# Transposing k, v and r by DMA instead of by matmuls from the fifth chunk on, with the instruction order drawn up anew

One core of a Trainium2 chip. The metric is the device time of one execution in microseconds (us), lower is better. Runs are compared with runs of the kernel before on the same chip. A run is called slow when it is over 1.5% above the fastest run of its kernel, otherwise fast; medians below are over all runs, ratios over fast ones alone. The engines: PE does the matmuls, DVE, ACT and POOL the element-wise work and the copies, SP issues DMAs.

## What is computed

A linear-attention recurrence with a 40x40 state for each of 4 x 8 heads over 768 steps, followed by an MLP with a softplus on the 3072 resulting rows of 320:

```python
for t in range(S):                       # r, k, v, w, a, b: [4, 8, 768, 40] f32
    y[:, :, t] = einsum('bhd,bhde->bhe', r[t], state)
    Sa    = einsum('bhde,bhe->bhd', state, a[t])
    state = state * w[t][..., None] - einsum('bhd,bhe->bhde', Sa, b[t]) \
                                    + einsum('bhd,bhe->bhde', v[t], k[t])
x = y.transpose(0, 2, 1, 3).reshape(3072, 320)
out = softplus(x @ w_in) @ w_out         # w_in 320x2048, w_out 2048x320
```

The kernel works in 12 chunks of 64 steps. In a chunk the recurrence becomes products of 64x64 blocks ("grams"), a triangular inversion (by DVE or POOL, one for two chunks) and a short chain on the state; the MLP of a chunk follows when its y is there.

## The kernel before

A small list scheduler in the program orders all operations by due times ("TUNED") on a cost model and then emits them, one in-order stream for each engine. The cut shows one chunk's transposes. `op(engines, reads, writes, fn)` enters an operation; `evac` copies PSUM to SBUF on ACT or DVE, whichever the scheduler picks.

```python
def transpose(src, srcs, t, off):            # 8 transposing matmuls of 128x128 into PSUM
    def f(e):
        for bp in X2:
            for yy in range(H_ // 2):
                i = T.transpose(pb(t)[:, bp, off + 128*yy:off + 128*yy + 128],
                                src[:, bp, 128*yy:128*yy + 128], ident[:, :])
        return i
    return op(pe(8 * 56.0), srcs + ["ident"], [t], f, mode=FULL, name="tr")
...
for n, dst, dn in (("v", v_, vn), ("r", r_, rn)):          # POOL casts f32 to bf16
    op(pool(640 * 0.85), landed(RAW[n], c), [dn], ...)
t = Tile("a")
transpose(k_, [kn], t, 0)
transpose(v_, [vn], t, 512)
evac(1024, [t], [kTn], lambda t=t: kT_[:], ...)
evac(1024, [t], [vTn], lambda t=t: vT_[:], ...)
t = Tile("a")
transpose(r_, [rn], t, 0)
evac(1024, [t], [rTn], lambda t=t: rT_[:], ...)
masked(grams(kT_, kTn, G, aT_, aTn, F), ta[:], tan)        # first readers
masked(grams(vT_, vTn, G, rT_, rTn, G), p_[:], pn)
...
op({"sp": 200.0}, [on], [...],                             # stores and most loads: SP
   lambda e, ...: S.dma_start(out[row:row + L, :], ot[q:q + 64, :]), ...)
```

kT, vT, rT and r_b have one buffer each, v_b two.

Of the kernel before, what the change touches and what calls it, by code (L numbers as in the profile page):

```python
# [17 lines left out]
NEAR = 4  # L18
GT = 8
DVE_FW = (0, 1)  # L20
FIRST = ["b2", "w0", "a0", "b1", "w2", "a1", "a2", "r3", "v3", "r1", "k0", "v2", "a3", "b3", "v1", "k2", "k1", "r0",
    "k3", "v0", "r2", "b0"]
BY_ACT = ("a2", "b0", "b1", "b2", "k3",)

DUE = {}
TUNED = {("const", 0): (-3.693, 1.677), ("logs", 0): (-8.629, 903.459), ("logs", 2): (3.218, 2.271),
    ("logs", 4): (9.161, 0.555), ("logs", 6): (1.81, 0.029), ("logs", 8): (3.58, 3.191),
    ("logs", 10): (1.467, 0.43), ("first", 0): (-6.199, 0.211), ("first", 1): (-2.981, 1.025),
    ("first", 2): (-2.078, 0.185), ("first", 3): (-1.533, 0.02), ("first", 4): (-3.465, 0.201),
    ("first", 5): (-3.012, 0.221), ("first", 6): (-3.897, 2.263), ("first", 7): (-3.262, 0.329),  # L30
    ("first", 8): (-1.395, 0.039), ("first", 9): (-5.529, 0.956), ("first", 10): (-1.743, 0.114),
    ("first", 11): (-2.881, 0.778), ("invert", 0): (-10.218, 0.059), ("invert", 1): (-5.518, 0.024),
    ("invert", 2): (-7.57, 0.518), ("invert", 3): (-3.213, 0.079), ("invert", 4): (-5.511, 0.134),
    ("invert", 5): (-2.481, 13.837), ("weights", 0): (1.187, 928.349), ("csb", 0): (0.548, 691.95),
    ("before", 0): (-5.516, 0.172), ("before", 1): (-0.859, 0.024), ("before", 2): (0.018, 0.026),
    ("before", 3): (0.176, 0.59), ("before", 4): (0.665, 1.484), ("before", 5): (0.314, 0.462),
    ("before", 6): (-3.434, 2.547), ("before", 7): (4.711, 1.26), ("before", 8): (1.286, 1.509),
    ("before", 9): (0.234, 0.102), ("before", 10): (-0.599, 50.77), ("before", 11): (-7.144, 0.037),
    ("W", 0): (11.058, 0.094), ("W", 1): (0.162, 0.089), ("W", 2): (3.065, 0.189), ("W", 3): (-2.415, 81.382),
    ("W", 4): (-4.831, 6.172), ("W", 5): (0.114, 0.183), ("W", 6): (-0.851, 0.546), ("W", 7): (11.05, 12.868),  # L40
    ("W", 8): (1.208, 0.442), ("W", 9): (-3.367, 3.578), ("W", 10): (3.873, 0.948), ("W", 11): (1.626, 0.28),
    ("chain", 0): (0.366, 0.103), ("chain", 1): (0.823, 0.27), ("chain", 2): (0.607, 0.021),
    ("chain", 3): (0.517, 0.239), ("chain", 4): (0.917, 0.02), ("chain", 5): (0.415, 0.364),
    ("chain", 6): (0.982, 0.194), ("chain", 7): (2.773, 0.063), ("chain", 8): (-0.307, 0.235),
    ("chain", 9): (-0.166, 1.763), ("chain", 10): (2.249, 0.247), ("chain", 11): (-1.862, 7.214),
    ("after", 0): (0.576, 0.02), ("after", 1): (-0.482, 1.399), ("after", 2): (0.383, 0.189),
    ("after", 3): (-3.78, 1.371), ("after", 4): (-7.952, 3.19), ("after", 5): (-2.305, 0.052),
    ("after", 6): (-4.679, 0.366), ("after", 7): (-0.275, 0.048), ("after", 8): (-0.196, 0.697),
    ("after", 9): (-3.747, 4.706), ("after", 10): (-1.685, 1.926), ("after", 11): (10, 1.373),
    ("mlp", 0): (0.936, 0.072), ("mlp", 1): (1.107, 1.432), ("mlp", 2): (0.768, 1.497),  # L50
    ("mlp", 3): (1.021, 1.422), ("mlp", 4): (0.453, 0.271), ("mlp", 5): (-0.453, 2.276),
    ("mlp", 6): (0.981, 0.601), ("mlp", 7): (1.01, 1.599), ("mlp", 8): (-2.424, 0.838),
    ("mlp", 9): (-2.927, 0.024), ("mlp", 10): (-6.757, 17.608), ("mlp", 11): (-3.21, 0.023),
    ("load w", 4): (-8.02, 13.468), ("load w", 6): (-4.853, 7.506), ("load w", 8): (-3.389, 9.625),
    ("load w", 10): (-5.349, 0.02), ("load a", 4): (2.419, 0.02), ("load a", 5): (5.777, 0.056),
    ("load a", 6): (-3.318, 0.081), ("load a", 7): (-0.465, 0.024), ("load a", 8): (-0.222, 0.269),
    ("load a", 9): (2.558, 1.896), ("load a", 10): (-5.461, 0.023), ("load a", 11): (0.774, 0.989),
    ("load b", 4): (-7.204, 0.118), ("load b", 5): (-0.103, 0.077), ("load b", 6): (-7.078, 0.203),
    ("load b", 7): (-2.54, 0.02), ("load b", 8): (-1.682, 0.02), ("load b", 9): (0.892, 6803.691),
    ("load b", 10): (-7.568, 0.102), ("load b", 11): (-8.196, 123.948), ("load k", 4): (-4.002, 0.086),  # L60
    ("load k", 5): (-5.178, 0.02), ("load k", 6): (-5.609, 0.045), ("load k", 7): (-7.576, 0.02),
    ("load k", 8): (-4.291, 0.278), ("load k", 9): (0.319, 112.278), ("load k", 10): (-3.896, 0.021),
    ("load k", 11): (-3.756, 1.782), ("load v", 4): (-0.823, 1.073), ("load v", 5): (-1.083, 0.84),
    ("load v", 6): (0.068, 1502.815), ("load v", 7): (-4.848, 1195058.862), ("load v", 8): (3.334, 2.238),
    ("load v", 9): (5.232, 4.558), ("load v", 10): (-3.373, 1248.895), ("load v", 11): (1.415, 186.217),
    ("load r", 4): (-1.133, 1.48), ("load r", 5): (-2.972, 0.39), ("load r", 6): (5.651, 4.768),
    ("load r", 7): (3.08, 0.625), ("load r", 8): (-1.475, 18.071), ("load r", 9): (6.571, 43.008),
    ("load r", 10): (9.094, 1220.994), ("load r", 11): (1.725, 0.138)}
NQ = DFF // 128
LN2 = 0.6931471805599453  # L70

# [92 lines left out]
LAT = {"pe": 240.0, "dve": 130.0, "act": 150.0, "pool": 130.0, "sp": 0.0}  # L164
SELF = 75.0
SWITCH = 150.0
PEN = 14.64
PERIOD = 25000.0
BETA = 0.29


BLOCK, AHEAD, FETCH, BEFORE = 256, 82, 2300.0, 70

PORT = ("scale", "fw")
SLOW = ("h", "o", "csb")
FILL, SAVE, MARGIN = 10072.17, 241245251.54, 6.88
COUNT = {"tr": 8, "tot": 16, "gram": 32, "cum": 8, "W": 32, "X1": 16, "X": 32, "D": 32, "U": 32,
         "S1": 4, "S": 64, "sT": 32, "y1": 16, "y": 64, "yT": 6, "h": 6, "o": 4, "csb": 16}

# [209 lines left out]
def bass_rwkv7_goose__then__act_softplus_kernel(  # L389
# [17 lines left out]
    with ExitStack() as st:  # L407
# [32 lines left out]
        def pb(t, lo=0, hi=1024):  # L440
            return psb[:, t.bank:t.bank + 2, lo:hi]
# [51 lines left out]
        csb = sb("csb", [128, DM], F32)  # L493
# [40 lines left out]
        def evac(cols, reads, writes, o, i, fast=False, name="", only=None):  # L534

            c = dict(dve(cols * (0.52 if fast else 1.04)))
            c.update(act(cols))
            if only:
                c = {only: c[only]}
            return op(c, reads, writes, lambda e: copy(e, o(), i()), name=name)  # L540
# [152 lines left out]
        def transpose(src, srcs, t, off):  # L693
# [4 lines that stand above are left out]
                        i = T.transpose(pb(t)[:, bp, off + 128 * yy:off + 128 * yy + 128],  # L698
                                        src[:, bp, 128 * yy:128 * yy + 128], ident[:, :])
                return i  # L700
            return op(pe(8 * 56.0), srcs + ["ident"], [t], f, mode=FULL, name="tr")

        def at(side, bp, x, yy):

            return bp, 128 * yy + side(bp, x)
# [87 lines left out]
        def first(c):  # L793
# [18 lines left out]
               lambda e: V.scalar_tensor_tensor(hd(n_), bh(bf_, D_), -1.0, bh(gi, D_), ALU.mult, ALU.mult), name="scale")  # L812
            op(dve(666), landed(RAW["k"], c) + [gin], [kn],
               lambda e: V.tensor_tensor(hd(k_), bh(kf, D_), bh(gi, D_), ALU.mult), name="scale")  # L814
            t = Tile("a")
            transpose(a_, [an], t, 0)
            evac(1024, [t], [aTn], lambda t=t: aT_[:], lambda t=t: pb(t, 0, 512), fast=True)
            t = Tile("a")
            transpose(n_, [nn], t, 0)
            evac(1024, [t], [nTn], lambda t=t: nT_[:], lambda t=t: pb(t, 0, 512), fast=True)  # L820
            td = grams(aT_, aTn, F, nT_, nTn, G, F)
            m, mn = mc(wd)
            z = c % 2
# [52 lines left out]
        def second(c):  # L876
# [34 lines left out]
            def pair(n):  # L911
                return [n + "b0", n + "b1"]


            for n, dst, dn in (("v", v_, vn), ("r", r_, rn)):
                src = RAW[n](c)[0]
                op(pool(640 * 0.85), landed(RAW[n], c), [dn],
                   lambda e, dst=dst, src=src: P.tensor_copy(hd(dst), bh(src, D_)), name="cast")  # L918
            t = Tile("a")
            transpose(k_, [kn], t, 0)  # L920
            transpose(v_, [vn], t, 512)
            evac(1024, [t], [kTn], lambda t=t: kT_[:], lambda t=t: pb(t, 0, 512), fast=True)
            evac(1024, [t], [vTn], lambda t=t: vT_[:], lambda t=t: pb(t, 512, 1024), fast=True)
            t = Tile("a")
            transpose(r_, [rn], t, 0)
            evac(1024, [t], [rTn], lambda t=t: rT_[:], lambda t=t: pb(t, 0, 512), fast=True)
            masked(grams(kT_, kTn, G, aT_, aTn, F), ta[:], tan)
            masked(grams(vT_, vTn, G, rT_, rTn, G), p_[:], pn)
            if not last:
# [116 lines left out]


            stage("after", c)
            t = Tile("a")
            transpose(u_, pair(un), t, 0)  # L1050
            evac(1024, [t], [uTn], lambda: uT_[:], lambda t=t: pb(t, 0, 512), fast=True)
            masked(grams(uT_, uTn, G, rT_, rTn, G), q_[:], qn)
            t = Tile("a")

# [135 lines left out]
```

## Time and profile before

| | before |
|---|---|
| median of its first 3 runs (lowest to highest) | 350.23 us (348.08 to 356.07) |
| span of the profiled run, mean granted PE clock | 351.7 us, 0.907 |
| PE, DVE, ACT, POOL busy | 274.8, 241.1, 210.9, 165.0 us |
| matmuls | 7632 |
| SP's time in issuing DMAs, all of it; from 160 to 200 us; 200 to 240 us | 221.6; 29.9 of 40; 24.6 of 40 us |

The lines of the profile that carry the argument stand in the prediction.

### The profile page before, as it was taken

What the parts mean: (1) busy time and instruction counts of PE and PEld (TensorE: products, weight loads), DVE (VectorE), ACT (ScalarE), POOL (GpSimd) and SP (SyncE); (2) the same over time, 40 slices, a digit from 0 to 9 for tenths busy, and PEclk for the clock granted to TensorE, in tenths of its full rate; (3) what the DMA queues carried; (4) which work ended last, traced back from release to release, by engine and by line L of the source; (5) the groups of instructions that cost most, each with busy time, mean ns of one, the idle gap of its engine ahead of it and who ended that gap; (6) DMA issues with size and microseconds to landing.
All of it is one profiled execution on the core that took longest, in us unless ns stands there. A gap on an engine that the chain in (4) does not pass through costs nothing.

```text
span 351.7 us, 16899 instructions
## 1 busy us (share of the span) xinstructions
PE 274.8 (78%) x7632; PEld 207.8 (59%) x7632; DVE 241.1 (69%) x475; ACT 210.9 (60%) x293; POOL 165.0 (47%) x294
## 2 busy tenths in 40 slices
PE   0641340558996989979999799979999999999883
PEld 0430220546775767757677587757777778777652
DVE  7950799999978977668668777657786646664201
ACT  1561201564694978946768587566777467746661
POOL 6030000010101079876999988877888988000000
PEclk9966565656599999999999999999999999999999
DMA  9999978657575664866515566222232220101011
GB/s 141 180 181 195 175 116 158 106 87 146 92 113 95 99 124 67 151 113 113 96 33 88 95 110 117 45 50 50 49 58 39 45 42 22 33 13 41 12 29 38
DMA packets 145737, 31.26 MB, mean 89 GB/s; under 512 B 140224, under 2 KB 145344, under 8 KB 145664
## 3 DMA queue, kind: packets, MB, share of 16 engines
q1 hardware_dynamic: 132672, 25.91, 44.6%
q0 software_dynamic: 2432, 2.62, 4.4%
q10 hardware_dynamic: 10560, 1.64, 3.6%
q8 instruction: 60, 0.98, 1.1%
q14 instruction: 13, 0.11, 0.1%
HBM read 28.84 MB, written 3.93 MB: 93 GB/s over the span
## 4 chain that ended last, share of the span: by engine, by line
PE 50%; DVE 16%; ACT 9%; POOL 8%; issue 6%; DMA 6%; SPq 3%; POOLq 1%; DVEq 0%; ACTq 0%
PE ps L1096 14%; PE ps L1115 11%; PE ps L698 7%; DMA k_f<-in_k_dram 4%; DVE mtmp L853 4%; DVE mt L857 3%; POOL mt L857 3%; PE ps L719 3%; POOL mtmp L853 3%; DVE mt L848 2%; PE ps L962 2%; ACT et L1102 2%; ACT gT L1105 2%; SPq L635 2%; PE ps L760 2%
## 5 line engine op out<-in xcount | busy, mean ns | idle before, releaser
L1102 ACT ACTIVATE et<-ps 128x512 f32<-128x512 f32 x96 | 57.2, 596 | 45.7 <-PE ps L1096 44.4
L1096 PE MATMUL ps<-xT,win 128*128 128x256 bf16 x576 | 80.7, 277 | 2.5 <-ACT et L1102 1.4
L853 POOL TENSOR_TENSOR mtmp<-mt 128x30 f32<-128x30 f32 (+14 forms) x120 | 63.6, 530 | 22.2 <-DVE mt L848 13.6
L857 POOL TENSOR_TENSOR mt<-mt,mtmp 128x30 f32<-128x30 f32 (+14 forms) x120 | 64.2, 535 | 8.5
L1115 PE MATMUL ps<-wout,gT 128*128 128x320 bf16 x384 | 63.8, 300 | 3.5 <-ACT gT L1105 2.6
L1096 PEld LDWEIGHTS ps<-xT,win 128*128 128x128 bf16 x576 | 51.3, 99 | 14.6 <-ACT et L1102 4.5
L1105 ACT ACTIVATE gT<-et,hln 128x1024 bf16<-128x1024 f32 x48 | 55.2, 1149 | 1.2
L1115 PEld LDWEIGHTS ps<-wout,gT 128*128 128x128 bf16 x384 | 34.3, 98 | 16.8 <-ACT gT L1105 3.8
L918 POOL CAST r_b<-r_f 128x640 bf16<-128x640 f32 x12 | 9.5, 789 | 52.5 <-DMA r_f<-in_r_dram 43.6
L1120 DVE TENSOR_TENSOR osb<-ps,csb 128x320 f32<-128x320 f32 x24 | 11.6, 484 | 22.0 <-PE ps L1115 22.0
L918 POOL CAST v_b<-v_f 128x640 bf16<-128x640 f32 x12 | 8.6, 718 | 32.8 <-DMA v_f<-in_v_dram 17.5
L698 PE MATMUL ps<-ident,ah 128*128 128x128 bf16 x96 | 8.2, 235 | 17.1 <-DVE ah L810 16.1
L853 DVE TENSOR_TENSOR mtmp<-mt 128x30 f32<-128x30 f32 (+14 forms) x60 | 20.4, 342 | 1.2
L857 DVE TENSOR_TENSOR mt<-mt,mtmp 128x30 f32<-128x30 f32 (+14 forms) x60 | 19.9, 335 | 1.3
L760 PE MATMUL ps<-lw,nexc 64*64 64x320 bf16 x96 | 8.0, 371 | 16.3 <-ACT lw L791 10.1
L731 DVE TENSOR_TENSOR qt<-ps,sut 128x1024 bf16<-128x1024 f32 x12 | 14.7, 1223 | 6.1 <-PE ps L719 5.8
L814 DVE TENSOR_TENSOR kh<-k_f,ginv 128x640 bf16<-128x640 f32 x12 | 10.2, 848 | 10.7 <-DMA k_f<-in_k_dram 10.7
L698 PEld LDWEIGHTS ps<-ident,ah 128*128 128x128 bf16 x96 | 6.4, 105 | 18.7 <-DVE ah L810 17.4
L532 ACT ACTIVATE nT<-ps 128x1024 bf16<-128x1024 bf16 x9 | 9.2, 1022 | 13.6 <-PE ps L698 13.5
L698 PE MATMUL ps<-ident,nh 128*128 128x128 bf16 x96 | 8.4, 234 | 11.3 <-DVE nh L812 9.9
L1071 DVE TENSOR_TENSOR yo<-ps,gexc 128x640 bf16<-128x640 f32 x12 | 9.9, 824 | 9.3 <-PE ps L1065 9.3
L731 DVE TENSOR_TENSOR tak<-ps,sut 128x1024 bf16<-128x1024 f32 x12 | 14.6, 1216 | 1.8 <-PE ps L719 1.6
(132 smaller groups left out, 566.3 us busy)
## 6 DMA issues: line engine op xcount, KB each, us to landing
w_f<-in_w_dram SPq DMA_DIRECT2D x24, 160.0 KB, 3.8
r_f<-in_r_dram SPq DMA_DIRECT2D x48, 80.0 KB, 3.5
v_f<-in_v_dram SPq DMA_DIRECT2D x48, 80.0 KB, 3.4
out_dram<-osb SPq DMA_DIRECT2D x48, 80.0 KB, 2.6
a_f<-in_a_dram SPq DMA_DIRECT2D x44, 80.0 KB, 3.7
k_f<-in_k_dram SPq DMA_DIRECT2D x44, 80.0 KB, 3.3
b_f<-in_b_dram SPq DMA_DIRECT2D x36, 80.0 KB, 3.2
wout<-in_moe_w_out_dram POOLq DMA_DIRECT2D x1, 1280.0 KB, 14.9
```

Of the source, the lines that this page charges most:

```text
L698: i = T.transpose(pb(t)[:, bp, off + 128 * yy:off + 128 * yy + 128], src[:, bp, 128 * yy:128 * yy + 128], ident[:, :])
L719: i = T.matmul(pf(t)[o:o + 64, hp, c:c + L], lhs[q:q + D_, lh, lc:lc + L], rhs[q:q + D_, rh, rc:rc + L])
L731: lambda e: V.tensor_tensor(parity(dst), bh(pf(t), L), bc4(mask[:, :], L), ALU.mult), name="mask")
L760: i = T.matmul(pf(t)[s:s + 64, bp, 0:DM], mats[z][q:q + 64, :], heads(lwt[q:q + 64, bp, :], 2 * D_)[:, :, z * D_:z * D_ + D_], start=(z == ...
L853: lambda e, j=j, nt=nt, tv=tv: E_.tensor_tensor(tv, m[:, 0:j, j:j + 1].to_broadcast([128, j, nt]), m[:, j:j + 1, j + 1:32].to_broadcast([1 ...
L857: lambda e, j=j, tv=tv: E_.tensor_tensor(m[:, 0:j, j + 1:32], m[:, 0:j, j + 1:32], tv, ALU.add),
L918: lambda e, dst=dst, src=src: P.tensor_copy(hd(dst), bh(src, D_)), name="cast")
L1096: i = T.matmul(one(t)[:, 256 * (q % 2):256 * (q % 2) + 256], win[:, z, q * 128:(q + 1) * 128], xT_[:, z, :], start=(z == 0), stop=(z == 2))
L1102: lambda e, q2=q2, t=t, ett=ett: A.activation(ett[:, q2 % 2, :], one(t), AF.Exp), name="exp")
L1105: lambda e, q2=q2, ett=ett: A.activation(gts[q2 // 2][0][:, :, :].rearrange("p q m -> p (q m)"), ett[:, :, :].rearrange("p q m -> p (q m)" ...
L1115: i = T.matmul(one(t)[:, 0:DM], gts[z][0][:, q % 4, bp * 128:(bp + 1) * 128], wout[:, q, :], start=(q == 0), stop=(q == NQ - 1))
L1120: lambda e, t=t, ot=ot: V.tensor_tensor(ot[:], one(t)[:, 0:DM], csb[:], ALU.add), name="oe")
```

## The change

Intent: PE is the busiest engine in the middle of the kernel (37.4 to 39.0 of 40 us from 200 to 320 us); take 24 groups of 8 transposing matmuls and 24 PSUM copies away, and give the work to the DMA engines, which are at least half idle there (share 0.15 to 0.46). k, v and r of chunks 4 to 11 go from SBUF to SBUF by a DMA transpose that SP issues. The scheduler's due times, its constants and the order of the first loads were searched for anew.

```diff
+BY_DMA = {"k": 4, "v": 4, "r": 4, "u": 99, "a": 99, "n": 99}
+        def transpose_dma(src, sn, dst, dn):
+            op({"sp": 1350.0}, sn, [dn],
+               lambda e: S.dma_start_transpose(
+                   out=dst[:, :, :].rearrange("p b (y m) -> p (b y) m", m=128),
+                   in_=src[:, :, :].rearrange("p b m -> p (b m)")), dma=("tr" + dn, 1230))
+        def turned(c, *ts):          # by DMA where c >= BY_DMA[...], else by matmuls as before
...
-            transpose(k_, [kn], t, 0)
-            transpose(v_, [vn], t, 512)
-            evac(...)  # kT, vT
+            turned(c, ("k", k_, [kn], kT_, kTn), ("v", v_, [vn], vT_, vTn))
-            transpose(r_, [rn], t, 0)
-            evac(...)  # rT
+            turned(c, ("r", r_, [rn], rT_, rTn))
... all entries of TUNED, and FIRST, BY_ACT, PEN, BETA, FILL, SAVE, MARGIN: new values
```

## The prediction, as put on record

The 220 ns and 56 ns in it are times of the 128x128 transposing matmuls.

> **What bounds the kernel now.** I read the busy tenths by slice first, then busy time per stretch, then the PE and POOL timelines, then the waits of the SP queue and the DMA issues.
>
> ```profile
> PE   0641340558996989979999799979999999999883
> DVE  7950799999978977668668777657786646664201
> POOL 6030000010101079876999988877888988000000
> PEclk9966565656599999999999999999999999999999
> DMA  9999978657575664866515566222232220101011
> ```
>
> A slice is 8.8 us. Three parts are to be seen. To about slice 14 (125 us) DVE is the full row (it does the first two of the six inversions), the loads fill the DMA row and the PE clock is half. From there to slice 36 PE is the full row at full clock, with POOL second, which does the last four inversions. The last 30 us are the tail of the MLP, with PE waiting on ACT.
>
> ```profile
> core 0: us, PE busy (x) PEld busy (x) DVE busy (x) ACT busy (x) POOL busy (x), PEclk, DMA share, GB/s
> 40.00:80.00 40.00, 16.90 (x364) 12.09 (x362) 37.61 (x94) 14.44 (x19) 2.88 (x4) 0.59 0.77 122
> 200.00:240.00 40.00, 37.40 (x1054) 28.44 (x1054) 28.85 (x42) 28.39 (x43) 33.84 (x60) 1.00 0.46 79
> 240.00:280.00 40.00, 38.96 (x1230) 29.43 (x1225) 28.23 (x42) 27.26 (x40) 34.52 (x62) 1.00 0.25 47
> 280.00:320.00 40.00, 38.96 (x1171) 30.91 (x1170) 24.02 (x40) 26.76 (x37) 16.93 (x31) 1.00 0.15 31
> ```
>
> In the middle PE is busy 37.4 to 39.0 of 40 us, ACT and DVE 24 to 29, the DMA engines 15 to 46%. So PE time is what a change must save, and DMA time is cheap there. Chunks 4 to 11, the ones changed, have nearly all their k, v and r transposes in that middle part.
>
> POOL is the second limit. Its closing instruction of an inversion (the masked copy to mb) starts at these times:
>
> ```profile
> 209.71 2.87 POOL L862 TENSOR_TENSOR mb<-mt,fmask 128x1024 bf16<-128x1024 f32 x1
> 255.85 2.83 POOL L862 TENSOR_TENSOR mb<-mt,fmask 128x1024 bf16<-128x1024 f32 x1
> 296.15 2.80 POOL L862 TENSOR_TENSOR mb<-mt,fmask 128x1024 bf16<-128x1024 f32 x1
> ```
>
> They are 46.1 and 40.3 us apart, for two chunks each. The work in one is (63.6 + 64.2) / 4 = 32.0 us for the two element-wise groups, 2.8 for this copy and four casts of 0.72, together 37.7. So POOL does not go much below 40 us a pair. Its first inversion starts at 123.9 us and the kernel ends 53 us after the last.
>
> [...] The trace shows 220 ns for one matmul of these, and in a row they come every 56 ns, as shown below; the pipelined figure is what PE pays. [...]
>
> **The change part by part: what is removed.** Three transposes in each of 8 chunks, 24 groups of 8 matmuls. This is the PE timeline of one chunk at full clock, with starts in the first column:
>
> ```profile
> 310.92 0.29 PE L962 MATMUL ps<-state,rT 40*64 40x40 bf16 x11
> 311.14 0.62 PE L698 MATMUL ps<-ident,r_b 128*128 128x128 bf16 x8
> 311.69 0.44 PE L1065 MATMUL ps<-kh,pt 64*64 64x40 bf16 x32
> ...
> 293.11 0.62 PE L698 MATMUL ps<-ident,kh 128*128 128x128 bf16 x8
> 293.57 0.61 PE L698 MATMUL ps<-ident,v_b 128*128 128x128 bf16 x8
> 294.02 0.82 PE L1096 MATMUL ps<-xT,win 128*128 128x256 bf16 x6
> ```
>
> The second column overlaps with the next row, so I take differences of starts: k 0.46, v 0.45, and r 0.55, which stands between groups in 64x64 mode. Thus 1.46 us a chunk and 8 x 1.46 = 11.7 us of PE. The instruction orders give nearly the same: 192 fewer transposes at 0.056 us are 10.7, and the changes between 128x128 and 64x64 mode fall from 144 to 126, some 0.1 us each (0.55 less 0.45), 1.8 more: 12.5. Of the two I take **12 us**.
>
> Off PE, 24 copies from PSUM go (1024 columns, 1022 ns on ACT or 690 on DVE): about 20 us from two engines with 11 us of 40 to spare. That is worth little directly, but a copy no longer stands between other work of the chain, and each frees a PSUM pair earlier.
>
> **What is added.** 24 transposes of 128x1024 bf16, 256 KB each. [...] The issue on SP costs the scheduler's own assumption of 1.35 us. Landing comes on top: a store of 80 KB from SBUF lands in 2.6 us and a load in 3.4.
>
> ```profile
> v_f<-in_v_dram SPq DMA_DIRECT2D x48, 80.0 KB, 3.4
> out_dram<-osb SPq DMA_DIRECT2D x48, 80.0 KB, 2.6
> ```
>
> So from a free SP to a usable tile I estimate 1.35 + 3 = 4.5 us, against 1.7 us before (0.45 on PE, 0.2 of signals, 1.02 of copy). [...]
>
> Whether 4.5 us is hidden, I read from the new instruction order. kT, vT and rT have one buffer each, so a transpose may start only after the previous chunk's last reader on PE. Adding up PE work at the trace's durations between that reader and the next first use, k has 12 to 27 us (5.7 in chunk 11), v 6 to 30, and r 9.8, 11.6, 4.3, 10.5, 4.0, 6.9, 9.8 and 3.6 us in chunks 4 to 11. Before, r had 1.0 to 7.9. The scheduler has made the room, with three tight ones (chunks 6, 8 and 11), where I expect 1 to 2 us of waiting each: **+4 us** on PE, with one more for another place.
>
> **What is moved.** Everything: all due times, the order of the first 22 load groups, seven of them issued by ACT instead of five. The first 125 us, which are not PE's, may shift a few us either way. POOL's first inversion has one cast fewer in front of it, and DVE's transpose for it now stands ahead of a mask and a transpose (1.2 + 1.05 us) that it followed. For an order searched for anew on top of a freer PE I take **-4 us**, the least certain term; it is a choice, not a count.
>
> **Sum.** 350.2 - 12 + 4 - 4 = 338.
>
> **The rivals.** (a) POOL becomes the bound. A pair of chunks takes PE 40 us or so and POOL 38 to 40. With 2.9 us a pair taken off PE, POOL holds the pace: 123.9 + 4 x 40 + 53 = 337, if nothing starts earlier. For it: 34 of 40 us busy. Against it: the 53 us tail holds MLP work that could be done before, so it shrinks when PE is freer. It limits the gain to about 13 us rather than destroying it: 337 to 342.
>
> (b) A wait takes the place of the work. SP takes its instructions in order, and it already stands at stores for results not yet there:
>
> ```profile
> SPq L1125 <- DVE osb L1120: 42.4, 10, 8.6
> SPq L635 <- POOL mt L857: 22.4, 7, 7.2
> ```
>
> In the new order the first k transpose stands directly behind stores of the MLP's output. A transpose stuck there delays a gram on PE, and also POOL: the cast of the next r waits until the transpose has read r_b, in the middle of an inversion. If a third of the 24 are 2 us late, the gain shrinks by 16 us, to nothing: 345 to 352. Against it: stores were placed knowing this, and the windows above are mostly above 6 us.
>
> (c) The transpose is far slower. [...] PE would wait several us in most chunks: 355 to 375. Against it: [...] an author who set first chunk and cost per tensor must have seen transfers.
>
> (d) The new order is worth more than I think, because a freer PE and ACT let the head close earlier: 325 to 332. For it: the head has 125 us in which PE is mostly idle. Against it: the head hangs on DVE and loads, untouched here.
>
> **Range and chances.** The central 338 has rival (a) near it. (d) sets the low end, about 1 in 8; a mild (b) the high end, about 1 in 6; (c) I give 1 in 25. So 328 to 347. Faster by 2% is below 343.2: 0.76. Within 2%: 0.20. Slower: 0.04.
>
> **What would show each step.** Right: the groups of transposing matmuls into kT, vT, rT fall from 12 to 4 chunks, and PE busy falls by 11 to 14 us in all. Transpose issues appear on SP 24 times, landing in 2.5 to 4.5 us. PE waits on these DMAs, in total, 3 to 6 us. POOL's closing copies stand 39 to 42 us apart. The first POOL inversion starts at 118 to 124 us. Wrong: landing above 7 us (c); PE or POOL waits on transposes over 12 us (b); PE busy less by 12 but idle more by as much in the middle with POOL full (a, stronger than I hold); a first inversion 8 us earlier or later, which would mean that the reordering and not the transposes made the time.

## The result

370.6 us median (369.09 to 375.38, 4 runs, the highest of them slow) against 350.81 us (348.08 to 356.07, 4 runs) for the kernel before. The ratio is **1.058** (95% interval 1.048 to 1.068): slower by about 20 us, where 12 us less were predicted. Ratios here and below are the mean time of one kernel's fast runs over that of the other's of the same rounds, so not quite the ratio of the medians. One point of a ratio is 3.5 us.

The page of the kernel after, busy tenths by slice (a slice is 9.2 us):

```profile
PE   0272151457898987799889898789999989789883
DVE  7673399999889956756647565566776444363201
POOL 6040010000100589875858578778788698100000
PEclk9986585555589999989989899989999999898999
DMA  9999972777657644877587976585731785020011
```

The PE row has sevens and eights in its middle where it had nines, yet the kernel is longer, so PE's busy time in all is what it was, 274.0 against 274.8 us, in spite of 192 fewer matmuls. New are the eights in the PE clock row between slices 17 and 36 (counted from 0): before, it was all nines there. The DMA row is fuller: from 125 us on the share is 0.44 against 0.27. Busy time by stretch of the kernel after (columns: window, its length, PE, PEld, DVE, ACT, POOL, granted PE clock, DMA share, GB/s):

```profile
200.00:240.00 40.00, 34.68 (x1046) 26.30 (x1041) 24.40 (x34) 24.58 (x36) 30.51 (x58) 0.96 0.73 115
240.00:280.00 40.00, 37.34 (x967) 28.26 (x968) 28.01 (x40) 28.63 (x42) 32.29 (x57) 0.96 0.57 86
280.00:320.00 40.00, 34.65 (x1060) 25.73 (x1051) 20.11 (x30) 23.24 (x35) 28.39 (x49) 0.99 0.52 69
```

PE does less in each stretch and at a lower clock. POOL's closing copies, from its timeline, tell where the time was lost:

```profile
220.38 2.81 POOL L882 TENSOR_TENSOR mb<-mt,fmask 128x1024 bf16<-128x1024 f32 x1
268.57 2.82 POOL L882 TENSOR_TENSOR mb<-mt,fmask 128x1024 bf16<-128x1024 f32 x1
311.77 2.79 POOL L882 TENSOR_TENSOR mb<-mt,fmask 128x1024 bf16<-128x1024 f32 x1
```

The first one (166.90 us) still comes half a microsecond earlier than before's (167.41); the next three are later by 10.7, 12.7 and 15.6 us. Two thirds of the loss fall between 167 and 220 us. Most of that is not the transposes: the same order without them (e3 below) has these copies at 167.5 and 217.4 us, so it loses 7.6 of the 11.2 us by itself. The wait that stands out in the kernel after is nevertheless one that the change added. Waits of POOL after 125 us there (total, times, longest; 7.9 us of it between 160 and 222 us):

```profile
POOL r_b L938 <- DMA rT<-r_b: 15.2, 6, 4.0
```

The cast of the next r may not overwrite r_b until the transpose has read it. Waits of PE from 125 us on, before and then after (the two longest entries of each, and the only one for a transpose; "issue" is time for which the profile shows no wait):

```profile
PE ps L962 <- issue: 3.2, 4, 1.6
PE ps L1115 <- ACT gT L1105: 2.6, 3, 1.9
```

```profile
PE ps L976 <- issue: 5.7, 6, 1.7
PE ps L1053 <- issue: 4.1, 3, 1.9
PE ps L743 <- DMA rT<-r_b: 1.3, 2, 1.1
```

All of this list together: before, issue 7.6, waits for data 6.5, sum 14.1 us; after, issue 16.4, data 11.7, transposes 1.3, sum 29.4 us. So PE hardly waits on the transposes themselves; it stands idle 15 us more for other reasons. The issue pauses of 1 to 2 us end 1.3 to 1.6 us after a 16 KB packet of the instruction queue has landed, which I read as PE having run out of fetched instructions; the fetches themselves took about as long in both (1043 and 1096 ns on average from 125 us on). From 125 us on, such pauses of 0.9 us and more came three times in the kernel before (1.2 to 1.6 us) and nine times in the kernel after (0.9 to 1.9 us).

And PE's busy time from 125 us on did not fall, though 192 matmuls were gone. (In this stretch there are 100 fewer; 92 others, done earlier in the kernel before, now fall into it.) The windows of the kernel before and of the kernel after over that stretch:

```profile
125.00:420.00 295.00, 208.03 (x5974) 158.24 (x5971) 141.55 (x212) 151.57 (x214) 149.47 (x261) 0.99 0.27 49
```

```profile
125.00:420.00 295.00, 209.30 (x5874) 155.16 (x5866) 134.73 (x196) 146.27 (x213) 149.07 (x262) 0.96 0.44 70
```

The clock column gives a second part of the reason. The trace holds the granted clock in steps of 3.41 us, full or half. Before has no half step from 98 us to 350 us. After has six between 158 and 333 us, 20.5 us in all, each worth 1.7 us of lost PE time at most: 10 us, about what the removal saved. Each follows a pause of PE (1.1 to 1.9 us, measured as in the list of waits), as here:

```profile
155.10:158.50 3.40, 1.70 (x97) 1.61 (x97) 1.13 (x3) 1.79 (x3) 1.97 (x4) 1.00 0.91 160
158.50:161.90 3.40, 3.40 (x28) 1.50 (x30) 2.34 (x4) 1.32 (x3) 3.10 (x5) 0.50 0.78 143
```

In the first window PE is busy only half the time (1.7 us of it is one pause); in the next the clock is 0.50. Over all twenty traces, of the windows between 125 and 345 us that follow a full-clock window, 32 of 38 were halved where the one before held a PE pause of 1.6 us or more, and 1 of 959 where its longest pause was under 0.6 us (21 of 226 between). These counts shift by some tens with where a pause is taken to begin; the contrast does not. The kernel before has pauses of 1.73 and 1.82 us by this measure (1.6 in the list of waits) that were followed by no half window, so a pause is not enough by itself.

Last, SP. Three lines of its timeline in the kernel after (start, duration, count):

```profile
185.20 2.36 SPq L637 DMA_DIRECT2D v_f<-in_v_dram  x2
187.60 1.35 SPq L708 DMA_TRANSPOSE rT<-r_b  x1
188.99 2.30 SPq L708 DMA_TRANSPOSE kT<-kh  x1
```

A transpose holds SP for 1.23 to 2.4 us; 24 of them took 38.5 us, and SP issues DMAs for 262.0 us instead of 221.6: 37.6 and 38.1 of 40 us in the two stretches from 160 to 240 us where it had 29.9 and 24.6. SP is full in the middle, so what it issues can come late. What lands is quick enough (DMA issues of the kernel after, median us from issue to landing; for kT and vT the trace does not tell it here, in e1 it is 3.5 and 3.3):

```profile
out_dram<-osb SPq DMA_DIRECT2D x48, 80.0 KB, 2.9
v_f<-in_v_dram SPq DMA_DIRECT2D x44, 80.0 KB, 3.2
rT<-r_b SPq DMA_TRANSPOSE x8, 4.4
```

### The profile page after: what moved, and what is told of

The parts are those of the page before. It is cut to its first block, busy times and chain, and to the rows that moved or that the text cites. A ratio compares the mean times of both kernels' runs of the same rounds, so it can differ in the third digit from the quotient of the medians.

```text
span 368.1 us, 16520 instructions
## 1 busy us (share of the span) xinstructions
PE 274.0 (74%) x7440; PEld 203.5 (55%) x7440; DVE 233.7 (63%) x459; ACT 198.7 (54%) x285; POOL 165.2 (45%) x294
## 4 chain that ended last, share of the span: by engine, by line
PE 47%; DVE 21%; issue 8%; ACT 7%; ACTq 6%; POOL 5%; DMA 4%; POOLq 1%; DVEq 0%; SPq 0%
PE ps L1108 13%; PE ps L1127 11%; ACTq L637 6%; PE ps L700 5%; DVE mtmp L873 4%; DVE mt L877 4%; DMA rT<-r_b 3%; PE ps L743 3%; ACT gT L1117 2%; PE ps L784 2%; POOL mt L877 2%; POOL mtmp L873 2%; ACT et L1114 2%; PE ps L1010 2%; PE ps L976 2%
## 5 line engine op out<-in xcount | busy, mean ns | idle before, releaser
L1108 PE MATMUL ps<-xT,win 128*128 128x256 bf16 x576 | 84.4, 286 | 4.1 <-ACT et L1114 3.0
L873 POOL TENSOR_TENSOR mtmp<-mt 128x30 f32<-128x30 f32 (+14 forms) x120 | 63.8, 531 | 29.4 <-DVE mt L868 20.9
L1127 PE MATMUL ps<-wout,gT 128*128 128x320 bf16 x384 | 65.5, 305 | 5.3 <-ACT gT L1117 4.0
L1108 PEld LDWEIGHTS ps<-xT,win 128*128 128x128 bf16 x576 | 52.8, 101 | 18.1 <-ACT et L1114 5.7
L1132 DVE TENSOR_TENSOR osb<-ps,csb 128x320 f32<-128x320 f32 x24 | 11.7, 489 | 27.7 <-PE ps L1127 24.7
L851 ACT ACTIVATE mc<-ps,blk 128x512 f32<-128x512 f32 x12 | 8.3, 688 | 21.7 <-issue 17.9
L784 PEld LDWEIGHTS ps<-lw,nexc 64*64 64x64 bf16 x96 | 2.8, 124 | 30.2 <-ACT lw L815 16.0
L755 DVE TENSOR_TENSOR pt<-ps,sut 128x1024 bf16<-128x1024 f32 x12 | 14.7, 1223 | 6.8 <-PE ps L743 6.8
L700 PE MATMUL ps<-ident,nh 128*128 128x128 bf16 x96 | 9.5, 258 | 11.9 <-DVE nh L836 11.9
L853 DVE SCALAR_TENSOR_TENSOR mc<-ps,blk,mc 128x512 f32<-128x512 f32 x12 | 8.9, 744 | 12.6 <-ACT mc L851 12.6
```

The costliest lines, as they stand in the source:

```text
L700: i = T.transpose(pb(t)[:, bp, off + 128 * yy:off + 128 * yy + 128], src[:, bp, 128 * yy:128 * yy + 128], ident[:, :])
L755: lambda e: V.tensor_tensor(parity(dst), bh(pf(t), L), bc4(mask[:, :], L), ALU.mult), name="mask")
L784: i = T.matmul(pf(t)[s:s + 64, bp, 0:DM], mats[z][q:q + 64, :], heads(lwt[q:q + 64, bp, :], 2 * D_)[:, :, z * D_:z * D_ + D_], start=(z == ...
L873: lambda e, j=j, nt=nt, tv=tv: E_.tensor_tensor(tv, m[:, 0:j, j:j + 1].to_broadcast([128, j, nt]), m[:, j:j + 1, j + 1:32].to_broadcast([1 ...
L1108: i = T.matmul(one(t)[:, 256 * (q % 2):256 * (q % 2) + 256], win[:, z, q * 128:(q + 1) * 128], xT_[:, z, :], start=(z == 0), stop=(z == 2))
L1127: i = T.matmul(one(t)[:, 0:DM], gts[z][0][:, q % 4, bp * 128:(bp + 1) * 128], wout[:, q, :], start=(q == 0), stop=(q == NQ - 1))
```

## The experiments

Eighteen kernels. Each keeps the recorded order of one of the two kernels, instruction by instruction, and changes one thing in it. Four theories: **O**, the new order is the slower one; **W**, the transposes land late; **S**, their issue fills SP's queue; **C**, their bytes load the DMA engines and with them the instruction fetch. Later came **K**, the clock, and **B** against **D**, whether PE's work sets the pace or the chain of data. Where something was left out, old data were used; the comparison is blind to such data.

### Taking the change apart: e1, e5, e2, e3

```diff
 e1: before's order; 24 transposes by DMA on SP, as soon as source and buffer are free
-transpose(k_, ...); evac(...)           # chunks 4 to 11, also v and r
+S.dma_start_transpose(out=kT_..., in_=k_...)
 e5: before's order; 24 transposes taken away, nothing in their place
 e2: after's order;  24 transposes by matmuls and copies, at the DMA transposes' places
 e3: after's order;  24 transposes taken away
```

> The order of the kernel before, instruction for instruction, on every engine, with only the 24 transposes of k, v and r taken from PE and put on SP as DMA transposes, each where its source and its buffer are free. Theory O (the new order is at fault: it lets PE run out of fetched instructions among short matmuls, the gaps halve the clock, and the transposes by DMA are innocent): 336 to 346 us. Theory W (the 4.4 us to landing make PE and POOL wait): 355 to 370. Theory C (the transposes load the DMA engines, so that PE's instruction fetches come late): 355 to 370.

> The order of the kernel before with the 24 groups of transposing matmuls and their copies left out, and no DMA transposes in their place; the result is wrong on purpose. This is what the removal alone is worth. The prediction's step (12 us of PE, all of it on the path): 334 to 340 us. If POOL or SP sets the pace instead: 344 to 350.

> The order of the changed kernel kept, with the 24 DMA transposes replaced by matmul transposes and copies put at the same places in the order. O: 372 to 383 us, the changed kernel's 370 plus up to 12 of PE work. W and C: 348 to 360, since the waits on DMA transposes and their load are gone.

> The changed kernel, same order and same places of PE's instructions (within 2), with the 24 DMA transposes not issued and nothing waiting for them; the result is wrong on purpose. O: 363 to 370 us, the gaps of PE stay (16 us of idle PE after 125 us put down to issue in the changed kernel, 7.6 before). W and C: 342 to 352.

| kernel | median us | ratio to before (95%) | PE busy / idle after 125 us | half-clock after 100 us |
|---|---|---|---|---|
| e5 before's order, none | 353.66 | 0.996 (0.986 to 1.005) | 199.6 / 20.5 | 17.0 |
| e1 before's order, DMA | 365.44 | 1.045 (1.039 to 1.051) | 203.7 / 32.0 | 27.2 |
| e3 after's order, none | 357.32 | 1.021 (1.014 to 1.027) | 206.6 / 21.5 | 19.9 |
| after | 370.6 | 1.058 (1.048 to 1.068) | 209.3 / 29.4 | 23.9 |
| e2 after's order, matmuls | 387.96 | 1.108 (1.101 to 1.115) | 227.7 / 30.3 | 43.9 |

Only two of e5's four runs were fast. The last column counts half-clock steps that begin after 100 us, the one at the kernel's end too (before: 3.0).

Three results. First, taking the 24 groups and their copies away without any replacement gives nothing (e5; by the interval between 4.9 us less and 1.9 us more): the 12 us that I counted on do not come out. Second, the new order is slower than the old one without any transposes in either (e3 against e5: 2.5 points, 9 us): theory O holds for a part. (e3 lies between the ranges of both theories.) e2 points the same way, but it lies above the 372 to 383 expected even under O, and its matmuls stand where a DMA would, so its size says little. Third, the transposes themselves cost 4.9 points in the old order (e1 less e5) and 3.7 in the new (after less e3), 17 and 13 us. The account of the 20 us in points: removal -0.4, order +2.5, transposes +3.7, sum 5.8 (-1.5, +8.7 and +13 us). The sum is exact by construction, each of the last two terms has some 1.2 points of interval either way, and the split depends on the sequence: with the DMA transposes put in first, they cost 4.9 and the order adds 1.3 (after less e1).

In e5 the window from 125 us on shows where the removed work went; PE's busy time fell by 8.4 us (of the 267 matmuls fewer in it, 75 now come before 125 us), and the idle time rose by 6.4, of which 5.5 are waits for results of other engines (12.0 against 6.5):

```profile
125.00:420.00 295.00, 199.63 (x5707) 147.87 (x5705) 131.77 (x196) 141.35 (x200) 148.25 (x256) 0.98 0.26 47
```

In e1, PE's waits are direct, and the largest is for r:

```profile
PE ps L2623 <- DMA rT<-r_b: 10.2, 4, 5.0
```

### What the transposes cost beside PE: e4, e6, e7, e8

```diff
 e4: kernel before
+S.dma_start_transpose(out=dum..., in_=win...)   # 24 of the same size, read by nobody
 e6: kernel before
+S.dma_start(dum[j:j+1, :], win[j:j+1, 0, 0:32]) # 72 DMAs of 64 bytes
 e7: kernel after
-load("a", c); load("b", c)                      # chunks 5 to 11: 56 DMAs, 36 us of SP
 e8: kernel after
-r_b = Ring("r_b", 1, ...)
+r_b = Ring("r_b", 2, ...)
```

> The kernel before, same order, with 24 DMA transposes of 256 KB from a constant tile into a tile nobody reads added on SP between the first and the last inversion of POOL. C: 358 to 370 us, with the idle time of PE put down to issue rising from 7.6 to about 16 us. O and W: 349 to 354, since nothing waits for them.

> The kernel before, same order, with 72 DMAs of 64 bytes on SP at the places of the 24 added transposes, three for each, about 46 us of SP's issue time and next to no bytes. Theory S (what the added transposes cost is SP's time: it issues in order, and stores and loads behind them come late): 355 to 362 us, as with the 24 added transposes (358). Theory C (the bytes and packets of the transposes load the DMA engines): 348 to 352.

> The changed kernel, same order, DMA transposes in place, with the loads of a and b of chunks 5 to 11 left out (56 DMAs of 0.64 us on SP, 36 us, about what the transposes take); old data is used, the result is wrong on purpose. Theory S: 355 to 361 us, near the order without transposes (357). Theory W (the latency of the transposes, with one buffer of r_b and rT): 366 to 371, the waits on rT stay.

> The changed kernel, same order, with two buffers for r_b, so that POOL's cast of the next r does not wait for the transpose of this one (15.2 us of POOL waits in the changed kernel). If POOL's waits set the time: 353 to 360 us. If POOL is late only because PE and SP are: 366 to 371.

| kernel | median us | ratio to before (95%) |
|---|---|---|
| e4 before + 24 idle transposes | 357.94 | 1.023 (1.015 to 1.030) |
| e6 before + 72 tiny DMAs | 364.22 | 1.027 (1.018 to 1.036) |
| e7 after without loads of a, b | 365.05 | 1.037 (1.029 to 1.044) |
| e8 after with two r_b | 369.46 | 1.053 (1.045 to 1.061) |

e4: transposes that nobody waits for cost 2.3 points. e6: somewhat more issue time (0.59 us each at the median, 52 us in all) with next to no bytes costs 2.7. So C is not needed, and S is a cost of its own. Against C there is more: with the bytes of 24 transposes added, PE's issue pauses are 7.2 us in e4 and 5.7 in e1, no more than the 7.6 before. (e6's profiled run is a slow one; the ratio uses its two fast runs.) The mechanism can be seen in e4. SP's timeline, and then DVE's:

```profile
172.23 1.28 SPq L3053 DMA_DIRECT2D out_dram<-osb  x2
```

```profile
175.93 0.49 DVE L3048 TENSOR_TENSOR osb<-ps,csb 128x320 f32<-128x320 f32 x1 [5.88 <-DMA out_dram<-osb]
```

The same store in the kernel before:

```profile
163.94 1.94 SPq L1125 DMA_DIRECT2D out_dram<-osb  x2
```

DVE had written this MLP result at 161.0 us; its store stood in SP's queue behind twelve loads and a transpose, all without a pause of SP, and went out at 172.23, 8.3 us later than before. DVE wanted to write the same buffer again and waited 5.88 us for it (before, that write waited 0.40 us, and for PE); the copy of yb stood behind that on DVE, PE waited 3.8 us for it (to 177.5), and the PE clock was half from 176.1 us for 6.8 us. A store sent out 8.3 us later became a pause of four on PE.

e8 removes the wait that looked worst in the profile after, POOL's 15.2 us, and gains nothing that the interval can tell (1.053 against 1.058). POOL then waits for DVE and PE instead (28.6 and 10.6 us): a wait that is listed is not thereby a cost. e7 gives SP its time back and gains 2.1 points of the 5.8, between the two ranges expected; the kernel before gains 1.0 from the same (e12 below).

### Is PE the bound: e9, e10, e12, e16

```diff
 e9:  e5, and 8 one-column matmuls near each place where 8 transposes were
+T.matmul(ps[..., 500:501], ident[0:m, 0:m], ident[0:m, 0:1])
 e10: kernel before
-for bp in X2:  ...transpose...
+for _ in range(2):                    # chunks 4 to 11: each group twice
+    for bp in X2:  ...transpose...
 e12: kernel before
-load("a", c); load("b", c)            # chunks 5 to 11
 e16: e5 without these loads
```

> Like e5 (order of before, the 24 transposes of chunks 4 to 11 and their copies gone, nothing in their place, wrong on purpose), but 8 one-column matmuls stand near each removed group of 8 transposing matmuls, so that PE's count of instructions, and with it the places where its instruction fetches fall, are those of before. Results may be called correct or not; the time counts. If the 12 us of PE work that e5 removed were taken back by gaps of PE at instruction fetches that fell in worse places (theory G), this gives some 342 to 346, well under e5's 353.7 (ratio to before 0.97 to 0.985 against e5's 0.996). If PE's work is not what sets the pace of the middle at all (theory D: the data and POOL's inversions do), it stays at 350 to 354, a ratio of 0.99 to 1.01.

> The kernel before with each of the 24 groups of transposing matmuls of chunks 4 to 11 run twice over (the same result): 192 more matmuls at 0.056 us, 10.8 us more of PE work, nothing else. My prediction's premise (theory B: in the middle PE's time is the kernel's time, one for one) gives 350.8 + 10.8 = 361.6, ratio 1.03. Theory D (PE has slack, the data and POOL's inversions set the pace) gives 351 to 355, ratio up to 1.012. Between: PE shares the pace, and a microsecond of PE work is worth about half.

> The kernel before with the loads of a and b of chunks 5 to 11 left out (56 DMAs, some 36 us of SP's issue time; the old data are used, wrong on purpose). It measures what SP's queue costs the kernel before. If SP is a bound already before (theory S in its strong form), 341 to 346, ratio under 0.985. If SP at 70 per cent has enough room and only the addition of the transposes fills it, 348 to 352, ratio 0.99 to 1.0.

> Like e5 (order of before, the 24 transposes gone with nothing in their place), and the loads of a and b of chunks 5 to 11 left out as well (wrong on purpose). e5 gave 0.996 and leaving out the loads alone 0.99. If SP's queue was the second bound behind PE, which held e5 back, the two together give far more than the sum: 338 to 343, ratio 0.96 to 0.975. If they only add, 347 to 350, ratio 0.985 to 0.995, and what held e5 back is the chain of data and the clock.

| kernel | median us | ratio to before (95%) |
|---|---|---|
| e9 e5 + one-column matmuls | 355.55 | 1.003 (0.986 to 1.019) |
| e10 transposes twice | 361.69 | 1.032 (1.022 to 1.041) |
| e12 before without loads of a, b | 348.45 | 0.990 (0.980 to 1.000) |
| e16 e5 without loads of a, b | 350.82 | 1.003 (0.997 to 1.009) |

The windows of e10, e12 and e17 (which comes below) from 125 us on:

```profile
125.00:420.00 295.00, 217.48 (x6164) 168.43 (x6161) 142.07 (x212) 152.54 (x213) 149.21 (x260) 0.99 0.27 49
125.00:420.00 295.00, 203.80 (x5890) 155.06 (x5888) 139.49 (x209) 148.78 (x209) 148.24 (x254) 1.00 0.21 38
125.00:420.00 295.00, 200.13 (x5749) 149.07 (x5742) 133.19 (x198) 142.56 (x202) 145.96 (x253) 0.99 0.29 52
```

e10 is the sharpest: 10.8 us of PE work added cost 11 us (7.7 to 14.4), about one for one, as theory B says. e5 took as much away and gained nothing, as D says. One reading joins them: in the kernel before, PE and the chain of data end together. More PE work lengthens the sum; less of it lets PE run into waits for others. This reading is argued, not shown. e10 also delays each copy behind a doubled transpose, so it does not tell PE's load from a longer chain of data.

e16 rules out that SP was that other bound: with SP relieved and the transposes gone it is no faster than e5 or e12, and it missed both ranges expected. The rival is the clock: half-clock windows (17.0 us after 100 us in e5, 19.3 in e16; before, 3.0 at the very end) can eat up to 7 or 8 us. A pair speaks against the clock as the whole reason: e17 has 16 of the 24 groups off PE and only 6.0 us of half clock, most of it at the end, and is no faster than e12, which has all of them on PE (0.989 and 0.990; PE's idle time from 125 us on is 17.1 against 11.1 us). SP does issue 19 us more in it than in e12. In e5 the share of the clock stays open.

e9 is inconclusive on its question, the places of the instruction fetches: a one-column matmul cost PE about 45 ns ((208.2 - 199.6) us / 192, from a slow run's profile), so that PE had about as much work as before. Its interval is too wide, 1.4 points below 1 to 1.9 above, to tell more than that the 24 PSUM copies, also gone, were not worth over some 5 us.

### Is the clock a cause: e13, e14

```diff
 kernel before, at 8 (e13) or 32 (e14) places of the dense part
+nc.vector.wait_ge(sem["pe"], n)
+V.memset(idle[:], 0.0)                # e13: five writes of 256 columns, e14: one of 1 column
+nc.tensor.wait_ge(gap, m)
```

> The kernel before, with 8 pauses of PE spread over its dense part: PE waits for DVE to write a spare tile five times, an estimated 2.0 to 2.5 us each, some 18 us in all (DVE has 11 us of 40 to spare). The result is right. Theory K (after a PE pause of 1.6 us or more the next 3.4 us window of the PE clock is halved, which costs 1.7 us more for each pause; it is what ate the saved matmuls in the changed kernel): halved windows appear after most of the 8 pauses, 20 us and more of them in all, and the time is the pauses plus 8 to 13 us: 372 to 382. If the halved windows have another cause (the order, the DMA load, chance), there are no more than two of them and the time is 350.8 plus the pauses, 364 to 370.

> The control of the long pauses: 32 pauses of PE in the same stretch, each for one tiny write on DVE, an estimated 0.4 to 0.5 us, some 14 us in all. Theory K: no halved windows beyond one or two, and the time is 350.8 plus the pauses (about 360 to 366). If idle time of PE as such brings the halved windows, there are as many here as with the long pauses.

e13: 370.21 us, 1.057 (1.048 to 1.067). e14: 359.63 us, 1.027 (1.021 to 1.034). In e13 the eight pauses were 2.1 to 2.7 us long, and six of them were followed at once by a half window; windows of e13, then the same stretch of the kernel before:

```profile
144.40:147.90 3.50, 1.15 (x10) 0.69 (x7) 2.97 (x8) 2.32 (x4) 3.11 (x6) 1.00 0.66 111
147.90:151.30 3.40, 3.30 (x64) 2.51 (x66) 0.69 (x1) 0.94 (x2) 0.25 (x1) 0.50 0.77 122
```

```profile
144.40:147.90 3.50, 3.50 (x65) 2.70 (x64) 3.08 (x6) 3.39 (x6) 3.15 (x5) 1.00 0.85 144
147.90:151.30 3.40, 3.23 (x139) 2.39 (x139) 2.40 (x5) 1.80 (x3) 3.12 (x6) 1.00 0.67 106
```

PE does 64 matmuls at half clock where it did 139 at full. e14, with 32 short pauses, has no half window before the very end (granted clock 1.00 from 125 to 345 us, 0.95 in e13; PE waits on the spare tile for 11.3 us in 31 entries, the longest 1.3 us). So long pauses do bring half-clock windows, and 32 short ones did not: K is shown as the cause of these windows. Its size was overestimated. PE's busy time after 125 us rose by 6.2 us (208.0 to 214.2), as six windows of 1.7 us at most allow. Its idle time rose by only 13.2 us (14.1 to 27.3), less than the 18 us of pauses, because other idle time shrank. Together that is about the 20 us that the kernel lost, below the 372 to 382 that I expected. In the kernel after, the 10 us of half-clock time are an upper limit of what the clock cost, not its share of the 20.

### Latency or issue: e11, e15, e17, e18

```diff
 e11: e1 with the queue of the transposes changed
-S.dma_start_transpose(...)
+A.dma_start_transpose(...)            # ACT issues them
 e15: e1, r by matmuls again
-BY_DMA = {"k": 4, "v": 4, "r": 4, ...}
+BY_DMA = {"k": 4, "v": 4, "r": 99, ...}
 e17: e15 without the loads of a and b of chunks 5 to 11
 e18: e1 without these loads
```

> Like e1 (order of before, the 24 transposes by DMA), but issued by ACT instead of SP at the same places; ACT has lost the copies from PSUM it made before. SP's queue is then that of before. Theory S (the transposes' issue fills SP's queue and delays stores and loads) gives back most of e1's 5 points: 354 to 358, ratio 1.01 to 1.02, unless ACT's own work is delayed as much by some 36 us of issue. Theory W (what costs is the landing time of 4 us between source and use) gives e1's 365, ratio 1.045, again with PE waiting 10 us and more on these DMAs.

> Like e1 (order of before, transposes by DMA on SP), but only k and v, 16 transposes; r by matmuls as before. In e1, PE waited 10.2 us on rT, 3.7 on kT and nothing on vT. Theory W (the landing of the late ones is the cost): falls from 1.045 to about 1.015, some 356. Theory S (SP's issue time, two thirds of it left): about 1.03, 361. If the two tight places of k cost as much as all of r, it stays near 1.04.

> Like e15 (order of before, k and v by DMA, ratio 1.026), but without the loads of a and b of chunks 5 to 11 (wrong on purpose): SP issues 16 transposes more and 56 loads fewer than before, so its queue is shorter than that of the kernel before. The kernel without transposes and without these loads (e16) gave 1.003. Theory S (what the k and v transposes cost is SP's issue time): 1.00 to 1.01, 351 to 354. If their cost is something else (the landing, the order of the waits, the clock), it stays at 1.02 to 1.03.

> Like e1 (order of before, all 24 transposes by DMA, ratio 1.045), but without the loads of a and b of chunks 5 to 11. Theory S alone: 1.005 to 1.015, 353 to 356. Theory W for r (10 us of PE waiting for rT, which lands too late however free SP is) on top of S for the rest: 1.02 to 1.03, 358 to 362. If SP's queue plays no part: 1.04 to 1.05.

| kernel | median us | ratio to before (95%) | PE waits on transposes |
|---|---|---|---|
| e1 k, v, r | 365.44 | 1.045 (1.039 to 1.051) | 13.9 us |
| e11 the same, issued by ACT | 366.67 | 1.042 (1.031 to 1.053) | 3.1 us |
| e15 k, v | 358.57 | 1.026 (1.018 to 1.034) | 1.6 us |
| e18 k, v, r, without loads | 357.14 | 1.014 (1.007 to 1.021) | 6.3 us |
| e17 k, v, without loads | 348.56 | 0.989 (0.984 to 0.995) | 0 |

For k and v: PE hardly waits on them (1.6 us), yet they cost 3.0 points over e5; with SP relieved the whole cost is gone (e17), and the kernel stands where e12 does, which has no DMA transposes. That is theory S. A caution on sizes: e16 does strictly less than e17 and is 1.4 points slower, with 19.3 us of half clock against 6.0, so differences of about a point between these kernels do not add up. With r, e18 keeps 2.5 points over e17 however free SP is: that is theory W, some 9 us (PE waits 6.0 us for rT; up to 7 us can be half clock, 20.4 us against 6.0); 3.1 points of e1 went with SP's loads (1.0 of them the kernel before gains from it too, e12). e11 missed: moving the issue to ACT freed SP but put the cost on ACT. PE's wait for ACT's `et` rose to 6.7 us over 10 times (kernel before: 1.4 over 3) and POOL's waits to 32 us (before: 7). That run suggests that the issue time costs on either queue; it does not tell what latency costs.

No version was found that beats both kernels and is right: e12 and e17 use old data.

## Why the prediction was wrong

**Removal, -12 us.** This is the step that failed first. The count was right: 7632 to 7440 matmuls, the groups gone. "So PE time is what a change must save" was not: e5 saves exactly this and its time changes by -0.4 points (-1.5 us; between -4.9 and +1.9). I had taken a PE row of 37 to 39 busy microseconds out of 40 for a bound that holds in both directions. e10 shows that added work costs its full time, e5 that removed work gives nothing back; why (PE then waits for other engines, 5.5 us more in e5) is in part argued. I put "PE busy less by 12 but idle more by as much" down as a sign of rival (a); it is what e5 shows in part (8.4 less, 6.4 more), with POOL's closing copies 44.5, 44.1 and 40.0 us apart, no closer than before and not at the 38 to 40 that I worked out for POOL.

**Waits on the transposes, +4 us.** The term is +13 us in the new order. The landing was estimated well (4.5 us; rT measured 4.4), and PE waits on transposes for only 1.3 us. (How much of the DMA engines' time they take, no run had shown: the packets of SP's queue q1 took 38 us more of the engines' time in e1 than before, 53.3% of 365.7 against 44.6% of 351.7 us, an estimated 1.6 us for each transpose.) What I did not count is SP's own time: I read "1.35 us" as a latency of each transpose, not as 38 us of load on a queue that was 221.6 us busy already. The profile has no busy row for SP, and I did not add it up. e4, e6, e15 and e17 show this part in the old order; e1 and e18 the late landing of r.

**Order, -4 us.** The term is +9 us (e3 against e5; by the intervals some 5 to 13). I called it a choice; its sign was wrong. Why the searched order is worse on the chip is only partly seen: in e3, POOL begins its second inversion 4.3 us after it is free, waiting for a copy on DVE, where the order before has that inversion begun ahead of the closing copy of the one before (the kernel after waits 3.3 us there). The search's model does not have the half clock. That this led it astray is argued, not shown.

**Sum.** -12 + 4 - 4 became -1.5 + 13 + 8.7, that is +20, against +20 measured; it must be, since the three terms are differences along one row of kernels.

**Rivals.** (b) had the right mechanism, SP in order (in e4 a store behind twelve loads and a transpose went out 8.3 us later) and POOL held up by r_b, and its sign came true (POOL waits 15.2 us on transposes, over the 12 named), but its range stopped at 352, and that wait is not the cost (e8). (c), slow transfers, an estimate that no run had shown, was wrong in its reason: they land in 4.4 us; its range of 355 to 375 held the result by another way. (d) was wrong. The first inversion of POOL starts at 123.0 us, inside the 118 to 124 predicted, and the head is not where the time went.

**What stays open.** How much of the 13 us in the new order is SP and how much is landing (e7 returns 7 us by relieving SP, of which the kernel before would gain half as well; e8 none that is sure by relieving POOL); how much the half clock costs in the kernel after and in e5; why the searched order is slower; and why some pauses bring no half window.

## What to carry to other kernels

Before work is moved to a DMA, add up the issue time on the queue that will carry it: an engine that the busy rows do not show can be 68% full (here from 160 to 240 us), and a transpose took 1.6 us of issue on average against some 0.64 for a load (median). An engine that is 95% busy (PE here, 37.4 to 39.0 of 40 us) need not be a bound for what is taken away: here added work cost its full time and removed work gave nothing, and doubling the work and leaving it out are two cheap runs that tell. Keep PE's pauses short where it is dense: here those under 0.6 us brought a half window once in 959, and those of 1.6 us and more cost half the clock of the next 3.4 us in 32 of 38.
